# Attention's loads of q and keys issued by ScalarE, instead of SyncE, while q, k and v are made

## The chip, the core and the metric

The kernel runs on one core of one Trainium2 chip. A core has five engines with a program of their own each: TensorE (PE: matrix products into PSUM; its weight loads are the rows PEld), VectorE (DVE), ScalarE (ACT), GpSimd (POOL) and SyncE (SP), which only issues DMAs. An engine takes its instructions strictly in the order of its program. ACT and POOL issue some DMAs as well; such an issue stands in the engine's own program (ACTq, SPq in the profile), together with the waits that the issue needs. The metric is the time of one execution in microseconds, as the median of several runs.

## The reference

With x of 2048 positions by 640 features, float32 throughout:

```
xn  = layernorm(x)
qkv = xn @ wqkv                       # 640 x 1920; 32 heads of 20
logits[s, w] = q[s] . k[s - 2 w] / sqrt(20),  w = 0..7,  masked where s - 2 w < 0
o   = sum_w softmax_w(logits)[s, w] * v[s - 2 w]
s   = o @ wo                          # 640 x 640
g   = silu(((xn @ w_gate) * (xn @ w_up)) @ w_down)      # 640 -> 1536 -> 640
out = x + s * g
```

## The kernel before, in words

Products in float32 are made of three products of split values (a high part, rounded, and a low part), so that each tile of q, k, v takes 15 matmuls (three parts by five slices of 128 features). A split needs an instruction on ACT (line L114) and one on POOL (L115). PE does the products of all stages one behind the other; the other engines work beside it.

The 32 heads are cut into six groups of 6, 6, 4, 4, 6 and 6 heads, and the positions into two interleaved halves (`r` = 0, 1). A group of heads on one half of the positions is a *unit* of attention, `u = 2 * group + r`, twelve in all; they are worked off in the order 0, 1, 2, 3, 4, 6, 5, 7, 8, 11, 9, 10. Making q, k, v goes through five stages (`MADE`: the groups 0, 1, 2 with 3, 4, 5), eight tiles of 128 positions to a half. Function `qkv` makes one tile: 15 matmuls (L434) into a PSUM bank, then an *eviction* by ACT (L448) into a staging buffer (`s`, or `pk`); after every second tile, one DMA (L452) writes the buffer to a scratch tensor in HBM, `qkv_scr` of that unit, four such writes to a unit. From stage 1 on, ACT issues these writes. A matmul group may only begin in a bank when the last result in that bank has been evicted. While attention runs, the banks take turns: `q_one` (rows `q`), then one of two banks `g`, then one of two banks `u`. So `q_one` comes up again after three products, each `g` and `u` bank after six.

Attention is the generator `attention`, which DVE (products and sums: L542, L549, L508), POOL (sums of weighted values: L514) and ACT (the exponential L571, a copy of q L498) work off. A unit's data come from `qkv_scr` by DMAs: `load_kq(u)` loads q (L414) and the keys (L420, and two shifted parts, L422); `load_kv(u, 1)` loads the values in the same way. The keys are loaded one unit ahead: `ahead(n + 1, (0,))` asks for them as soon as the code that emits the program has emitted the last write of that unit. q has one buffer, `kv` two.

The order on every engine is that in which this code emits instructions; `advance` decides, by a budget of estimated times, how many steps of attention are emitted behind each product of another stage. Each DMA of SP and ACT takes one of eight completion semaphores in turn (`DMAHW0` to `DMAHW7` below) and waits first until the DMA before it on that semaphore has landed, whichever engine issued it.

Of the kernel before, what the change touches and what calls it, by code (L numbers as in the profile page):

```python
# [22 lines left out]
W, DIL = 8, 2  # L23
# [33 lines left out]
def kernel(  # L57
# [11 lines left out]
    nc = tc.nc  # L69
# [13 lines left out]
    def st(shape, tag, bufs, dt=F32):  # L83
        cnt[0] += 1
        pool = sb
        if tag == "gh":
            pool, bufs = gh_pool
        return pool.tile(shape, dt, tag=tag, bufs=bufs, name=f"{tag}_{cnt[0]}")
# [50 lines left out]
    def load_wq(g, parts, ahead={}):  # L139

        c3 = 3 * MC[g]
        wq_raw.setdefault(g, [])
        for p in parts:
            t = st([P, p[-1] - p[0], c3], "wraw", 2)
            for k0, k1 in zip(p, p[1:]):
                if k0 in ahead:
                    ahead[k0]()
                nc.sync.dma_start(t[:, k0 - p[0]:k1 - p[0]], wqkv[g][:, k0:k1, :])
                wq_raw[g].append((k0, k1, t[:, k0 - p[0]:k1 - p[0]]))
# [3 lines left out]
    def split_wq(g, eng, ks=(0, KD)):  # L153
        c3 = 3 * MC[g]
        if not fifth:
            fifth.append(slot([P, 4, 3 * 128]))
        if g not in wq and MC[g] > CMAX:
            y = [slot([P, 3, CH])[:, :, :c3] for _ in range(4)]
            wq[g] = [[y[n // 3][:, n % 3] for n in range(a * KD, a * KD + KD)] for a in range(2)]
            wq[g].append(None)  # L160
        elif g not in wq:
            cols = -(-c3 // 64) * 64
            hi, lo = (slot([P, KD - 1, cols])[:, :, :c3] for _ in range(2))
            wq[g] = [[y[:, k] for k in range(KD - 1)] + [fifth[0][:, g % 2 * 2 + a, :c3]] for a, y in enumerate((hi, lo))]
            wq[g].append((hi, lo))
        for k0, k1, t in wq_raw[g]:
            for a, b in ((k0, min(k1, KD - 1)), (max(k0, KD - 1), k1)):
                a, b = max(a, ks[0]), min(b, ks[1])
                if a < b:
                    if b - a > 1:  # L170
                        hi, lo = (y[:, a:b] for y in wq[g][2])
                    else:
                        hi, lo = (y[a].unsqueeze(1) for y in wq[g][:2])
                    split(eng, t[:, a - k0:b - k0], hi, lo)
# [3 lines left out]
    def load_wf(f):  # L178
        wf_raw[f] = slot([P, KD, 2, P], F32) if f == 0 else st([P, KD, 2, P], "wraw", 2)
        nc.sync.dma_start(wf_raw[f], wgu[f])  # L180
# [201 lines left out]
    q_t, kv_t, kv_buf, kv_zero, scr, staged, made = {}, {}, {}, {}, {}, [], set()  # L382

    def view_kv(u, b):

        c = GROUPS[UN[u][0]] * DH
        if b not in kv_buf:
            y = st([P, -(-2 * EXT * CMAX // 64) * 64], "kv", 2)
            kv_buf[b] = y[:, :2 * EXT * CMAX].rearrange("p (a x) -> p a x", a=2)
        kv_t[u] = kv_buf[b][:, :, :EXT * c].rearrange("p a (e c) -> p a e c", c=c)  # L390

    def zero_kv(u, b, a):

        if kv_zero.get((b, a)) != GROUPS[UN[u][0]]:
            nc.gpsimd.memset(kv_t[u][0:1, a, 0:W - 1, :], 0.0)
            kv_zero[b, a] = GROUPS[UN[u][0]]

    def begin_unit(m, r):
        for g in MADE[m]:
            u, c = 2 * g + r, GROUPS[g] * DH  # L400
            if u:
                scr[u] = dr.tile([P, 3, NE, c], F32, name=f"qkv_scr_{u}")
            else:
                q_t[u] = st([P, NE, c], "q", 1)
                view_kv(u, r)
                for a in range(2):
                    zero_kv(u, r, a)

    def load_kq(u):

        c, b = GROUPS[UN[u][0]] * DH, ORDER.index(u) % 2
        view_kv(u, b)
        q_t[u] = st([P, NE, c], "q", 1)
        nc.sync.dma_start(q_t[u], scr[u][:, 0])  # L414
        load_kv(u, 0)

    def load_kv(u, a):

        zero_kv(u, ORDER.index(u) % 2, a)
        nc.sync.dma_start(kv_t[u][:, a, W - 1:, :], scr[u][:, 1 + a])  # L420
        for p0, p1 in ((0, 112), (112, 127)):
            nc.sync.dma_start(kv_t[u][p0 + 1:p1 + 1, a, 0:W - 1, :], scr[u][p0:p1, 1 + a, 1:, :])  # L422

    ALL_RUNS = [(a, b, k) for a, b in ALL3 for k in range(KD)]

# [256 lines left out]
    def finish_piece():  # L682

        while unfinished:
            unfinished.pop(0)()
# [74 lines left out]
    def wd_sum(n):  # L760

        t = {name: w_scr[:, i] for i, name in enumerate(("T1", "T2", "T3", "T4"))}
        if n == 0:
            for name, b in (("T1", "B11"), ("T3", "B12"), ("T2", "B22"), ("T4", "B21")):
                nc.sync.dma_start(t[name], wd_block(b))
        else:
            out, y = ((t["T1"], wd_block("B12")), (t["T3"], wd_block("B22")), (t["T2"], t["T1"]), (t["T4"], t["T2"]))[n - 1]
            nc.gpsimd.dma_start(out, y, accum_op=ALU.add)
# [367 lines left out]
    def t_unit(j, a, k, c0=2):  # L1136

        if j == "T4":
            return xT[c0 + 1][a][:, k, :]
        n, i = T_UNIT[j, a, k] if c0 else divmod(T2_UNIT[j, a] + k, 3)  # L1140
        while len(tt[c0]) <= n:
            tt[c0].append(slot([P, 3, CH]))
        return tt[c0][n][:, i]

    def load_t(n):

        tt[0].append(slot([P, 3, CH]))
        nc.gpsimd.dma_start(tt[0][n], t_scr[:, 3 * n:3 * n + 3])
# [36 lines left out]
    def last_difference(k):  # L1185
        y = t4.pop(k)
        nc.scalar.activation(t_unit("T4", 0, k), y, AF.Copy)
        nc.gpsimd.tensor_sub(t_unit("T4", 1, k), y, t_unit("T4", 0, k).bitcast(F32))

    def step(n=1):  # L1190

        while n and steps:
            if next(steps[0], 0) == 0:
                steps.pop(0)
            else:
                n -= 1
# [18 lines left out]
    def w_split(f, *names):  # L1215

        for t in names:
            to, r = t, slice(0, W_ROWS[t])
            if t in "GU":
                y = wf_raw[f][:, :, "GU".index(t), :]  # L1220
                if t == "U" and two(f):
                    to, r, y = "R", slice(3, 6), y[:, 2:]
            else:
                y = w_sum[f][:, 6 * "SR".index(t):][:, :6 if t == "S" else 3]
                r = slice(0, 6 if t == "S" else 3)
            w_unit(f, {"G": "A11", "U": "A22", "S": "S1", "R": "S4"}[t])
            split(nc.gpsimd, y, tw[to][:, 0, r], tw[to][:, 1, r])
# [116 lines left out]
    def first_parts():  # L1344
        for name in ("S1", "S2", "S3", "d5", "S4"):
            w_add(2, name)
            yield
        w_split(2, "S")
        yield
# [6 lines left out]
    for m, t in ((m, t) for m in range(1, len(MADE)) for t in range(DIL)):  # L1356
        r = t if m < last else DIL - 1 - t
        begin_unit(m, r)
        heads, broad = MC[m] // DH, m < last and MC[m + 1] > CMAX
        for i in range(NE):  # L1360
            n = t * NE + i
            if m < last and n == 0:
                load_wq(m + 1, ((0, 2), (2, 4)) if broad else ((0, 3), (3, 5)))
            elif m < last and n in BLOCK:
                split_wq(m + 1, nc.gpsimd, (BLOCK.index(n), BLOCK.index(n) + 1))
            elif broad and n == BLOCK[1] + 1:
                load_wq(m + 1, ((4, 5),))
            if (m, r, i) == (last - 1, 1, 6):
                load_wf(2)
            if (m, n) in W_SUMS:  # L1370
                wd_sum(W_SUMS.index((m, n)))
            qkv(m, r, i)
            if m == last and n == NT - 7:
                staged[:] = [y for y in staged if y is not stage_pk[-1]]
            elif m == last and n == NT - 5:
                load_t(0)
            elif m == last and n == NT - 3:
                w_split(2, "G")
            if i == 1:
                finish_piece()  # L1380
            advance(PACE * heads * 0.38)
            paced += RATE[m - 1][t]
            while paced >= 1:
                paced -= 1
                step()
        if (m, r) == (last - 1, 1):
            steps.append(first_parts())
        elif (m, r) == (last, 1):
            for k in range(2):
                last_difference(k)  # L1390
    step(100)
    w_split(2, "R")
    w_sum.pop(2)
# [237 lines left out]
```

## Time and profile before

| | before |
|---|---|
| median of 3 runs (lowest to highest) | 736.02 us (735.68 to 736.02) |
| the profiled execution: its own time, its span from first to last instruction | 736.29 us, 734.4 us |
| PE busy, share of span | 728.2 us, 99% |
| DVE, POOL, ACT busy | 626.5, 450.5, 302.2 us |
| granted TensorE clock | 1.000 |
| DMA queue of SP (q1) / of ACT (q10) | 121.13 MB / 12.78 MB |

In a timeline row stand the start and the length in us, the engine, the source line, the operation, the tile written and those read, their sizes, and in brackets the idle time of the engine before it and what ended that. `SPq` and `ACTq` are DMA issues: their length is that of the issue, and the transfer follows. "To landing" is counted from the start of the issue to the completion.

### The profile page before, as it was taken

What the parts mean: (1) busy time and instruction counts of PE and PEld (TensorE: products, weight loads), DVE (VectorE), ACT (ScalarE), POOL (GpSimd) and SP (SyncE); (2) the same over time, 40 slices, a digit from 0 to 9 for tenths busy, and PEclk for the clock granted to TensorE, in tenths of its full rate; (3) what the DMA queues carried; (4) which work ended last, traced back from release to release, by engine and by line L of the source; (5) the groups of instructions that cost most, each with busy time, mean ns of one, the idle gap of its engine ahead of it and who ended that gap; (6) DMA issues with size and microseconds to landing.
All of it is one profiled execution on the core that took longest, in us unless ns stands there. A gap on an engine that the chain in (4) does not pass through costs nothing.

```text
span 734.4 us, 11062 instructions
## 1 busy us (share of the span) xinstructions
PE 728.2 (99%) x4030; PEld 666.0 (91%) x4030; DVE 626.5 (85%) x729; ACT 302.2 (41%) x561; POOL 450.5 (61%) x383
## 2 busy tenths in 40 slices
PE   8999999999999999999999999999999999999997
PEld 6989989988999998888888888888999999999997
DVE  7676998798796989899889999969899997777775
ACT  5668312323232333333233322334566664444442
POOL 6159919997779889797879969766644550000000
PEclk9999999999999999999999999999999999999999
DMA  8564588789767669462733542376768965555534
GB/s 325 170 204 158 208 303 300 239 256 257 190 193 164 220 204 323 141 180 87 221 88 105 177 141 68 80 218 183 208 211 241 315 236 194 194 194 194 194 108 143
DMA packets 106148, 143.78 MB, mean 196 GB/s; under 512 B 23048, under 2 KB 75524, under 8 KB 106094
## 3 DMA queue, kind: packets, MB, share of 16 engines
q1 hardware_dynamic: 88366, 121.13, 52.0%
q10 hardware_dynamic: 16000, 12.78, 5.4%
q0 software_dynamic: 1728, 9.18, 5.1%
q8 instruction: 31, 0.51, 0.3%
q14 instruction: 23, 0.19, 0.1%
HBM read 94.40 MB, written 55.67 MB: 204 GB/s over the span
## 4 chain that ended last, share of the span: by engine, by line
PE 98%; DMA 1%; DVE 0%; SPq 0%; ACT 0%; issue 0%
PE g L1292 16%; PE u L1292 11%; PE q L434 11%; PE q L866 9%; PE u L434 8%; PE g L434 8%; PE u L866 6%; PE q L1292 5%; PE u L124 5%; PE g L124 5%; PE q L996 3%; PE g L866 3%; PE e L866 3%; PE u L996 2%; PE e L996 2%; PE g L996 1%
## 5 line engine op out<-in xcount | busy, mean ns | idle before, releaser
L514 POOL TENSOR_TENSOR o<-o,t 128x960 f32<-128x960 f32 (+1 forms) x66 | 133.7, 2025 | 11.3 <-DVE t L508 10.1
L508 DVE TENSOR_TENSOR t<-e,kv 128x960 f32<-128x960 f32 (+1 forms) x96 | 99.6, 1038 | 21.1 <-POOL o L514 21.1
L542 DVE TENSOR_TENSOR t<-q,kv 128x1920 f32<-128x1920 f32 (+1 forms) x48 | 92.4, 1926 | 2.8 <-DMA kv<-qkv_scr 2.7
L549 DVE TENSOR_REDUCE lg<-t 128x96 f32<-128x1920 f32 (+1 forms) x48 | 92.3, 1923 | 0.2
L434 PE MATMUL q<-s,xc 128*128 128x360 f32 (+1 forms) x450 | 82.8, 334 | 0.5 <-DVE lg L272 0.5
L1261 ACT ACTIVATE gh<-g 128x512 f32<-128x512 f32 x57 | 34.2, 600 | 109.0 <-PE g L1292 108.1
L434 PEld LDWEIGHTS q<-s,xc 128*128 128x128 f32 x450 | 74.8, 188 | 4.6 <-DVE lg L272 0.7
L115 POOL TENSOR_TENSOR s<-wraw,s 128x384 fp32r<-128x384 f32 (+6 forms) x57 | 68.0, 1209 | 17.5 <-ACT s L114 17.5
L434 PE MATMUL u<-s,xc 128*128 128x360 f32 (+1 forms) x360 | 65.8, 334 | 0.0
L434 PEld LDWEIGHTS u<-s,xc 128*128 128x128 f32 x360 | 60.3, 188 | 2.3
L434 PE MATMUL g<-s,xc 128*128 128x360 f32 (+1 forms) x330 | 61.5, 337 | 0.0
L434 PEld LDWEIGHTS g<-s,xc 128*128 128x128 f32 x330 | 55.7, 188 | 2.6
L1292 PE MATMUL g<-s,s 128*128 128x512 f32 x228 | 57.9, 389 | 0.0
L1292 PE MATMUL u<-xc,s 128*128 128x512 f32 x228 | 57.9, 389 | 0.0
L866 PE MATMUL q<-xc,s 128*128 128x320 f32 x342 | 55.5, 309 | 0.0
L866 PEld LDWEIGHTS q<-xc,s 128*128 128x128 f32 x342 | 51.5, 188 | 0.0
L1292 PEld LDWEIGHTS g<-s,s 128*128 128x128 f32 x228 | 42.8, 188 | 8.9
L1292 PEld LDWEIGHTS u<-xc,s 128*128 128x128 f32 x228 | 42.8, 188 | 8.9
L114 ACT ACTIVATE s<-wraw 128x384 fp32r<-128x384 f32 (+6 forms) x58 | 32.6, 581 | 29.4 <-PE g L1292 10.2
L1292 PE MATMUL q<-xc,pk 128*128 128x512 f32 x171 | 41.9, 389 | 0.0
L1292 PE MATMUL g<-xc,s 128*128 128x512 f32 x171 | 41.9, 389 | 0.0
L514 POOL TENSOR_TENSOR o<-t 128x960 f32<-128x960 f32 (+1 forms) x11 | 22.1, 2011 | 27.4 <-DVE t L508 22.7
(328 smaller groups left out, 1559.7 us busy)
## 6 DMA issues: line engine op xcount, KB each, us to landing
h_scr<-gh SPq DMA_DIRECT2D x48, 256.0 KB, 2.8
wraw<-in_wgu SPq DMA_DIRECT2D x11, 640.0 KB, 4.8
kv<-qkv_scr SPq DMA_DIRECT2D x14, 480.0 KB, 6.1
t<-h_scr SPq DMA_DIRECT2D x8, 768.0 KB, 6.3
qkv_scr<-s ACTq DMA_DIRECT2D x17, 360.0 KB, 4.4
kv<-qkv_scr SPq DMA_DIRECT2D x14, 367.5 KB, 7.1
s_scr<-gh SPq DMA_DIRECT2D x16, 320.0 KB, 3.6
gh<-s_scr SPq DMA_DIRECT2D x16, 320.0 KB, 4.1
```

What stands on the lines that cost most here:

```text
L114: nc.scalar.activation(hi, raw, AF.Copy)
L115: eng.tensor_sub(lo, raw, hi.bitcast(F32))
L124: nc.tensor.matmul(acc, a, b, start=first and n == 0, stop=last and n == len(runs) - 1)
L434: nc.tensor.matmul(p, xT[(r * NE + i) // TPC][a][:, k, t0:t0 + P], wq[m][b][k], start=n == 0, stop=n == len(runs) - 1, skip_group_check=ac ...
L508: nc.vector.tensor_mul(t.rearrange("p (n d) -> p n d", d=DH), e[:, :, w].unsqueeze(2).to_broadcast([P, NE * nh, DH]), v)
L514: return NE * c * cost, lambda: eng.tensor_add(y, z, t)
L542: nc.vector.tensor_mul(t, q, k)
L549: nc.vector.tensor_reduce(out=lg[:, :, j:j + 2].rearrange("p n a -> p a n"), in_=t.rearrange("p a (n d) -> p a n d", d=DH), op=ALU.add, ax ...
L866: nc.tensor.matmul(p, y[:, i, k], wd_part(name, k, l), start=new and r == 0, stop=r == len(runs) - 1, skip_group_check=True)
L996: nc.tensor.matmul(b, y, w, start=new and r == 0, stop=r == len(runs) - 1, skip_group_check=True)
L1261: nc.scalar.activation(kept[j], b["ACACABA"[j]], AF.Copy)
L1292: nc.tensor.matmul(y, w, x, start=j in (0, 1, 5) and r == 0, stop=r == len(runs) - 1, skip_group_check=True)
```

## The change

Until q, k and v of all units are made, `load_kq` issues its four DMAs (q, and three for the keys) from ACT; after that from SP, as before. The loads of values stay on SP.

```diff
         q_t[u] = st([P, NE, c], "q", 1)
-        nc.sync.dma_start(q_t[u], scr[u][:, 0])
-        load_kv(u, 0)
+        by[0].dma_start(q_t[u], scr[u][:, 0])
+        load_kv(u, 0, by[0])
 
-    def load_kv(u, a):
+    by = [nc.scalar]
+
+    def load_kv(u, a, eng=nc.sync):
...
-        nc.sync.dma_start(kv_t[u][:, a, W - 1:, :], scr[u][:, 1 + a])
+        eng.dma_start(kv_t[u][:, a, W - 1:, :], scr[u][:, 1 + a])
         for p0, p1 in ((0, 112), (112, 127)):
-            nc.sync.dma_start(kv_t[u][p0 + 1:p1 + 1, a, 0:W - 1, :], scr[u][p0:p1, 1 + a, 1:, :])
+            eng.dma_start(kv_t[u][p0 + 1:p1 + 1, a, 0:W - 1, :], scr[u][p0:p1, 1 + a, 1:, :])
...
+    by[0] = nc.sync
     step(100)
```

It moves 28 DMA issues, four each for the units 1, 2, 3, 4, 6, 5 and 7, from SP's program to ACT's. The programs of PE, DVE and POOL are the same row for row. Lines of the kernel behind the diff stand two or three further down afterwards (L448 becomes L450, L452 becomes L454).

ACT's program where q, k, v of unit 2 are done: `qkv_scr_1147` is that unit's scratch, `g_1322`, `u_1350` and `q_1_68` are products in the banks g, u and `q_one`, `s_1319` is a split of another stage. Before:

```order
L1166 ACTIVATE s_1319<-gh_1175 128x512 [waits Pool_49]
L448 ACTIVATE s_798<-g_1322 128x3x120 [waits PE_49]
L452 DMA qkv_scr_1147<-s_798 384x1x240 [waits DMAHW0_49,Activation_49]
L114 ACTIVATE s_1226<-wraw_1150 128x480
L448 ACTIVATE s_798<-u_1350 128x3x120 [waits DMAHW3_49,PE_49]
L448 ACTIVATE s_798<-q_1_68 128x3x120 [waits PE_49]
```

And now, on the same engine at the same place:

```order
L1168 ACTIVATE s_1319<-gh_1175 128x512 [waits Pool_49]
L450 ACTIVATE s_798<-g_1322 128x3x120 [waits PE_49]
L454 DMA qkv_scr_1147<-s_798 384x1x240 [waits DMAHW0_49,Activation_49]
L414 DMA q_1340<-qkv_scr_1147 128x960 [waits DMAHW3_49,DMAHW5_49,DMAHW1_49,DMAHW0_49]
L422 DMA kv_128<-qkv_scr_1147 128x960 [waits DMAHW2_49]
L424 DMA kv_128<-qkv_scr_1147 112x840
L424 DMA kv_128<-qkv_scr_1147 15x840 [waits DMAHW4_49]
L114 ACTIVATE s_1226<-wraw_1150 128x480
L450 ACTIVATE s_798<-u_1350 128x3x120 [waits PE_49]
L450 ACTIVATE s_798<-q_1_68 128x3x120 [waits PE_49]
```

The four loads stand directly behind the unit's last write and ahead of a split and two evictions; the first of them waits for the four writes of the unit (DMAHW0 is that of the write just above it).

SP's program at unit 1, whose scratch is `qkv_scr_771`; `h_scr` takes results of the gate and up products, `wraw` weights. Before:

```order
L672 DMA h_scr<-gh_1030 128x4x128 [waits DMAHW3_49,DVE_49]
L414 DMA q_1034<-qkv_scr_771 128x960 [waits DMAHW4_49,DMAHW2_49,DMAHW1_49]
L420 DMA kv_1033<-qkv_scr_771 128x960 [waits DMAHW6_49,DMAHW5_49]
L422 DMA kv_1033<-qkv_scr_771 112x840
L422 DMA kv_1033<-qkv_scr_771 15x840 [waits DMAHW7_49]
L672 DMA h_scr<-gh_1077 128x4x128 [waits DMAHW0_49,DVE_49]
L672 DMA h_scr<-gh_1102 128x4x128 [waits DVE_49]
L148 DMA wraw_1148<-in_wqkv 128x960 [waits Pool_49]
```

And now:

```order
L674 DMA h_scr<-gh_1030 128x4x128 [waits DMAHW4_49,DVE_49]
L674 DMA h_scr<-gh_1077 128x4x128 [waits DMAHW0_49,DVE_49]
L674 DMA h_scr<-gh_1102 128x4x128 [waits DMAHW1_49,DVE_49]
L148 DMA wraw_1148<-in_wqkv 128x960 [waits DMAHW2_49,Pool_49]
L148 DMA wraw_1150<-in_wqkv 128x960 [waits DMAHW3_49,Pool_49]
```

The store of `gh_1077` no longer stands behind the four loads of unit 1; on ACT these stand between the evictions `gh_1028` and `gh_1075` of the gate products.

## The prediction

> **What bounds the kernel now.** I read the page first, then the waits of PE.
>
> ```profile
> PE 728.2 (99%) x4030; PEld 666.0 (91%) x4030; DVE 626.5 (85%) x729; ACT 302.2 (41%) x561; POOL 450.5 (61%) x383
> PEclk9999999999999999999999999999999999999999
> PE 98%; DMA 1%; DVE 0%; SPq 0%; ACT 0%; issue 0%
> PE q L229 <- POOL lg masks.py:199: 1.4, 1, 1.4
> PE q L434 <- DVE lg L272: 0.5, 1, 0.5
> ```
>
> The first row is busy time by engine, the second the granted clock by slice, the third the shares of the chain that ended last, and the last two are all the waits of PE in the execution. PE is the chain, at full clock, and it waits for nobody but in its first microseconds. So a change on ACT and SP has nothing to shorten: SP's waits and ACT's idle time lie beside PE. What it can do is make PE wait where it did not, and as PE is dense to the end, such a wait is kept in full. The question is whether ACT, which now waits for loads' conditions in its own program, evicts a bank too late. The tightest bank is `q_one`, which comes up every third product.
>
> **Unit 2, the place that decides.** ACT's timeline, then SP's, then PE's:
>
> ```profile
> 122.40 0.47 ACT L448 ACTIVATE s<-q 128x360 f32<-128x360 f32 x1 [0.72 <-PE q L434]
> 129.19 0.63 ACT L1166 ACTIVATE s<-gh 128x512 fp32r<-128x512 f32 x1 [6.32 <-POOL gh L1162]
> 129.73 0.45 ACT L448 ACTIVATE s<-g 128x360 f32<-128x360 f32 x1
> 130.21 0.52 ACTq L452 DMA_DIRECT2D qkv_scr<-s  x1
> 130.78 0.60 ACT L114 ACTIVATE s<-wraw 128x480 fp32r<-128x480 f32 x1 [0.60 <-ACT s L448]
> 131.29 0.46 ACT L448 ACTIVATE s<-u 128x360 f32<-128x360 f32 x1
> 131.64 0.46 ACT L448 ACTIVATE s<-q 128x360 f32<-128x360 f32 x1
> ...
> 133.24 0.33 SPq L414 DMA_DIRECT2D q<-qkv_scr  x1
> 133.62 0.69 SPq L420 DMA_DIRECT2D kv<-qkv_scr  x1
> 134.36 0.92 SPq L422 DMA_DIRECT2D kv<-qkv_scr  x2
> ...
> 127.00 2.56 PE L434 MATMUL q<-s,xc 128*128 128x360 f32 x15
> 129.40 2.56 PE L434 MATMUL g<-s,xc 128*128 128x360 f32 x15
> 131.80 2.56 PE L434 MATMUL u<-s,xc 128*128 128x360 f32 x15
> 134.20 2.56 PE L434 MATMUL q<-s,xc 128*128 128x360 f32 x15
> ...
> DMA to landing us min/median/max: 3.0/3.0/3.0
> ```
>
> The last row is that of the write at 130.21: it lands at 133.2, and there SP issues the load of q, at 133.24. ACT is already late here: it stood 6.32 us for a sum of POOL, and catches up with three evictions in a row. The eviction of `q_one` ends at 131.64 + 0.46 = 132.10, and PE begins the next product in that bank at 134.20, so the slack is 2.10 us.
>
> Now the four loads stand behind the write at 130.21. ACT waits for the same landing, 133.24, and issues: on SP the four took from 133.24 to 134.36 + 0.92 = 135.28, 2.04 us. What began at 130.78 begins at about 135.33, 4.55 us later; the `q_one` eviction ends at 136.65 and PE starts at 136.65 rather than 134.20: **2.45 us of PE time lost**, 4.55 - 2.10. The bank `g` and `u` products in between have slack of six products and stay. The price of an issue on ACT is bounded by rows of its own: ACT's write above took 0.52, so four are 2.1; at SP's least, 0.33 each, 1.3. I take SP's 2.04 and keep -0.7 to +0.6 for the range.
>
> Behind the eviction, the exponential of attention comes some 2.8 us later too; DVE waited there anyway for keys, and PE has moved by about as much, so I cost it at nothing. If that cover goes, attention runs late; PE has no wait for it anywhere in the rows above.
>
> **Unit 1 sets when ACT gets there.** SP, ACT, DVE and POOL around it:
>
> ```profile
> 96.41 0.33 SPq L414 DMA_DIRECT2D q<-qkv_scr  x1
> 98.27 2.43 SPq L672 DMA_DIRECT2D h_scr<-gh  x2
> ...
> 95.40 0.60 ACT L657 ACTIVATE gh<-g 128x512 f32<-128x512 f32 x1 [6.20 <-PE g L124]
> 99.78 0.50 ACT L571 ACTIVATE e<-lg 128x384 f32<-128x384 f32 x1 [3.78 <-DVE lg L569]
> ...
> 95.19 0.68 DVE L668 TENSOR_TENSOR gh<-u,gh 128x512 f32<-128x512 f32 x1
> 103.08 2.16 DVE L542 TENSOR_TENSOR t<-q,kv 128x1920 f32<-128x1920 f32 x1 [1.12 <-DMA kv<-qkv_scr]
> 109.50 2.27 POOL L514 TENSOR_TENSOR o<-t 128x960 f32<-128x960 f32 x1 [14.80 <-DVE t L508]
> ...
> h_scr<-gh SPq DMA_DIRECT2D x48, 256.0 KB, 2.8
> kv<-qkv_scr SPq DMA_DIRECT2D x14, 480.0 KB, 6.1
> kv<-qkv_scr SPq DMA_DIRECT2D x14, 367.5 KB, 7.1
> q<-qkv_scr SPq DMA_DIRECT2D x7, 480.0 KB, 5.5
> ```
>
> ACT now stands until 96.4, when the last write of unit 1 has landed, issues until about 98.4, and evicts at 98.4 what it evicted at 95.40. That gate result lies in one of two `g` banks, and ACT is free at 99.0, before the exponential's 99.78: no cost. But SP no longer stands behind the loads: its store of the product that DVE ended at 95.87 goes out at 95.9, not at 98.27, beside the loads. DVE began unit 1 when these had landed, at 103.08, after 1.12 us of waiting, and POOL's chain up to the sum that ACT waits for at 129.19 starts from there. The loads are 1,328 KB in these rows, and took from 96.41 to 103, some 200 KB/us; 256 KB ahead of them cost up to 1.2 us, if all of it shares their time. At the other end, in a queue of their own, they could land sooner, of which DVE can use 1.12 us. I take +0.5, nearer to the first since the bytes are certain, and each microsecond counts in full at 134.20. That makes 2.45 + 0.5 = 2.95.
>
> **Unit 3, the other wait.**
>
> ```profile
> 145.17 0.52 ACTq L452 DMA_DIRECT2D qkv_scr<-s  x1
> 151.10 4.39 ACTq L452 DMA_DIRECT2D qkv_scr<-pk  x2
> 160.05 3.42 PE L434 MATMUL q<-s,xc 128*128 128x480 f32 x15
> DMA to landing us min/median/max: 11.6/11.6/11.6
> ```
>
> The last write of unit 3, at 145.17, landed after 11.6 us. The loads stand behind the two writes at 151.10, which go out about as before. With PE 2.95 later, the write is issued at about 147.6 and lands by 159.2; ACT is through with the issues at 161.3, has evicted `q_one` (0.57) by 161.9, and PE asks for the bank at 163.0. Slack 1.1 us: no cost, but near.
>
> **Units 4, 6, 5 and 7** are asked for in ACT's program behind the last write of their half, later than SP had issued the loads; the first and the last of the four, and DVE's first use of the last:
>
> ```profile
> 178.40 0.34 SPq L414 DMA_DIRECT2D q<-qkv_scr  x1
> 183.60 1.20 ACTq L452 DMA_DIRECT2D qkv_scr<-s  x2
> ...
> 255.18 0.34 SPq L414 DMA_DIRECT2D q<-qkv_scr  x1
> 263.70 0.52 ACTq L452 DMA_DIRECT2D qkv_scr<-s  x1
> 276.79 1.48 DVE L542 TENSOR_TENSOR t<-q,kv 128x1280 f32<-128x1280 f32 x1
> ```
>
> SP's conditions were met before ACT arrives, so these groups wait for nothing. Unit 7's loads slip by 12 us, to some 267 with PE 2.95 later, and need 5 to 7 us to land; DVE asks at 276.8. Four issues hold ACT for 2.04 us, while a `q_one` eviction has two products, 4.8 us. No cost. What SP gains, some 14 us of issuing and shorter queues for its stores, value loads and weights, has no waiter on PE: no gain. POOL's DMAs stay where they are.
>
> **Sum.** 2.45 + 0.5 = 2.95 us. The profiled execution took 736.29 (span 734.4), 0.27 above the median 736.02; on the median it gives **739.0 us**.
>
> **Rivals.**
> - *The stall is covered (not slower).* ACT is idle 59% of the time, and if it gets to unit 2's write earlier, the issues fit. Place: the 6.32 us wait for POOL ahead of 129.19. Price: loads of unit 1 in their own queue land 1.12 us sooner, and issues at SP's least take another 0.7 off: 2.45 - 1.8 = 0.6, 736.6. It decides where ACT's delay at the `q_one` eviction is under 2.1 + 1.5 us. Against it: SP's store now goes beside these loads.
> - *Only the issuer differs (not slower).* PE would show no wait and the time 736.0, if ACT held nothing back behind a waiting DMA. Against it: the row at 151.10, where two issues of ACT take 4.39 us. The Trainium skill has this as a rule, in "DMA: Bandwidth & Descriptors", section "Issuing engines are not separate DMA queues": DMAs of all engines run interleaved on the same 16 DMA engines, and the choice of issuer only saves its issue time, usually small. By that rule alone the change is worth nothing.
> - *Two stalls.* The write of unit 3 lands 2.6 us later than I have it (it then shares q10 with more loads): PE waits another 1.5 us, 740.5; with the upper ends at unit 2 (1.2 - 0.5 and 0.6) 741.8. The clock could add to it: "TensorE: Matmul & The Clock Gate", Part 1, in the Trainium skill, has the clock halved after an idle window of about 3.4 us; no run here shows it, and a gap of 2.95 is under it.
> - *Faster.* SP's earlier stores would have to end a wait of PE, and it has none after the start: 735 at best.
>
> **How the numbers follow.** One stall: 0.60, from 2.45 - 0.7 - 1.1 = 0.6 to 2.45 + 0.6 + 1.2 = 4.2 us, mostly within 737.5 to 740.2. The two covered rivals 0.09 each, two stalls 0.18, faster 0.04. A measurement can tell about 0.2%, 1.5 us. Slower by more: 0.56 of the first and the 0.18, 0.74; within: 0.04 and 0.18, 0.22; faster: 0.04. The range leaves out the lower covered cases and the upper part of two stalls: 736.5 to 741.5.
>
> **What would show it.** PE with one wait of 2 to 4 us for ACT's L450 at a product into `q_one` near 134; ACT with four issues behind the write near 130; PE's later rows shifted by the same amount; no waits at units 4 to 7. Wrong would be: PE without a wait, a second one near 163, or the wait of DVE at 103 gone.

## The result, and the profile after

| | before | after |
|---|---|---|
| median (lowest to highest) | 736.02 us (735.68 to 736.11, 4 runs) | 743.38 us (741.67 to 744.72, 4 runs) |
| the profiled execution: time, span | 736.29, 734.4 us | 744.14, 742.4 us |
| DMA queue of SP / of ACT | 121.13 / 12.78 MB | 113.14 / 20.77 MB |

The changed kernel is slower: ratio 1.010, 95% interval 1.0076 to 1.0123. The forecast of 739.0 us had the direction and the place, but 743.4 lies above its range (736.5 to 741.5).

The page of the kernel after (busy time), and all the waits of PE:

```profile
PE 732.5 (99%) x4030; PEld 669.8 (90%) x4030; DVE 628.1 (85%) x729; ACT 301.7 (41%) x561; POOL 451.5 (61%) x383
...
PE q L436 <- ACT s L450: 3.9, 1, 3.9
PE q L229 <- POOL lg masks.py:199: 1.4, 1, 1.4
PE q L436 <- DVE lg L272: 0.2, 1, 0.2
```

One wait of PE is new, 3.9 us for the eviction L450. But the span is 8.0 us longer, and PE's busy time grew by 4.3: about half of the loss isn't idle time, so a list of waits shows only the other half. PE's timeline at that wait, and seventy us later:

```profile
131.60 2.56 PE L436 MATMUL u<-s,xc 128*128 128x360 f32 x15
138.02 4.26 PE L436 MATMUL q<-s,xc 128*128 128x360 f32 x15 [3.86 <-ACT s L450]
142.07 2.69 PE L436 MATMUL g<-s,xc 128*128 128x360 f32 x15
...
204.02 2.63 PE L436 MATMUL q<-s,xc 128*128 128x360 f32 x15
206.49 2.63 PE L436 MATMUL g<-s,xc 128*128 128x360 f32 x15
```

From start to start, a product of 360 columns took 2.40 us in the kernel before (127.00, 129.40, 131.80). Here the one behind the gap begins 6.42 us after its predecessor, 4.02 too late; it takes 4.05 us (138.02 to 142.07), 1.65 too long; and all later ones take 2.47 (204.02 to 206.49), to the last of them. That is 164.4 ns for each matmul, not 160.0; with 35 products of 15 it makes 35 x 15 x 4.4 ns = 2.3 us. The sum is 4.0 + 1.65 + 2.3 = 8.0 us. The granted clock explains most of the second term (window in us, its length, then busy time of PE, PEld, DVE, ACT and POOL, PEclk, DMA share, GB/s):

```profile
136.00:138.00 2.00, 0.00 (x0) 0.00 (x0) 0.35 (x1) 1.32 (x3) 0.68 (x1) 1.00 0.85 292
138.00:139.00 1.00, 0.98 (x5) 0.99 (x6) 0.00 (x0) 0.44 (x1) 1.00 (x2) 0.89 1.02 417
139.00:140.00 1.00, 1.00 (x5) 1.00 (x5) 0.06 (x1) 1.00 (x4) 1.00 (x1) 0.50 1.07 330
140.00:142.07 2.07, 2.07 (x8) 2.07 (x8) 2.00 (x4) 0.82 (x2) 1.99 (x2) 0.50 0.67 203
142.07:144.60 2.53, 2.53 (x16) 2.53 (x16) 2.50 (x2) 0.47 (x1) 2.53 (x3) 0.98 0.64 209
```

The clock falls to half about 0.8 us after PE has started again, stays there for some 3.4 us, and is full afterwards: the slower 2.47 us are not the clock. The 40-slice row of the page still shows 9 everywhere; the dip is too short for it.

ACT's timeline at the place, to be held against the one of before:

```profile
130.17 0.63 ACT L1168 ACTIVATE s<-gh 128x512 fp32r<-128x512 f32 x1 [7.15 <-POOL gh L1164]
130.71 0.45 ACT L450 ACTIVATE s<-g 128x360 f32<-128x360 f32 x1
131.19 0.52 ACTq L454 DMA_DIRECT2D qkv_scr<-s  x1
134.80 0.35 ACTq L414 DMA_DIRECT2D q<-qkv_scr  x1
135.19 0.44 ACTq L422 DMA_DIRECT2D kv<-qkv_scr  x1
135.65 0.94 ACTq L424 DMA_DIRECT2D kv<-qkv_scr  x2
136.64 0.60 ACT L114 ACTIVATE s<-wraw 128x480 fp32r<-128x480 f32 x1 [5.48 <-issue]
137.15 0.45 ACT L450 ACTIVATE s<-u 128x360 f32<-128x360 f32 x1
137.50 0.46 ACT L450 ACTIVATE s<-q 128x360 f32<-128x360 f32 x1
```

It is the forecast stall: behind the write ACT waits 3.6 us for the landing, issues for 1.84 us, and evicts `q_one` by 137.96, while PE had been ready for that bank since 134.0.

### The profile page after: what moved, and what is told of

The parts are those of the page before. It is cut to its first block, busy times and chain, and to the rows that moved or that the text cites. A ratio compares the mean times of both kernels' runs of the same rounds, so it can differ in the third digit from the quotient of the medians.

```text
span 742.4 us, 11051 instructions
## 1 busy us (share of the span) xinstructions
PE 732.5 (99%) x4030; PEld 669.8 (90%) x4030; DVE 628.1 (85%) x729; ACT 301.7 (41%) x561; POOL 451.5 (61%) x383
## 3 DMA queue, kind: packets, MB, share of 16 engines
q1 hardware_dynamic: 85244, 113.14, 48.0%
q10 hardware_dynamic: 19122, 20.77, 8.6%
## 4 chain that ended last, share of the span: by engine, by line
PE 90%; DVE 3%; POOL 2%; DMA 2%; issue 1%; ACT 0%; SPq 0%; ACTq 0%; POOLq 0%; DVEq 0%
PE g L1294 16%; PE u L1294 10%; PE q L436 9%; PE q L868 9%; PE u L436 7%; PE g L436 6%; PE u L868 6%; PE q L1294 5%; PE u L124 3%; PE g L124 3%; PE q L998 3%; PE g L868 3%; PE e L868 3%; PE u L998 2%; PE e L998 2%; DVE lg L551 1%
## 5 line engine op out<-in xcount | busy, mean ns | idle before, releaser
L436 PE MATMUL q<-s,xc 128*128 128x360 f32 (+1 forms) x450 | 85.6, 341 | 4.1 <-ACT s L450 3.9
L436 PEld LDWEIGHTS q<-s,xc 128*128 128x128 f32 x450 | 77.0, 191 | 8.7 <-ACT s L450 4.1
L115 POOL TENSOR_TENSOR s<-wraw,s 128x384 fp32r<-128x384 f32 (+6 forms) x57 | 68.5, 1220 | 23.1 <-ACT s L114 23.1
L114 ACT ACTIVATE s<-wraw 128x384 fp32r<-128x384 f32 (+6 forms) x58 | 32.6, 581 | 35.0 <-issue 10.9
```

Source lines behind the costliest of these rows:

```text
L114: nc.scalar.activation(hi, raw, AF.Copy)
L115: eng.tensor_sub(lo, raw, hi.bitcast(F32))
L436: nc.tensor.matmul(p, xT[(r * NE + i) // TPC][a][:, k, t0:t0 + P], wq[m][b][k], start=n == 0, stop=n == len(runs) - 1, skip_group_check=ac ...
```

## The experiments

The eviction is line L448 of the kernel before, L450 of the changed one, and L451 or L459 in variants of it. The runs of before beside these had medians of 735.98 to 736.25 us.

**The change again, and its parts.** The changed kernel once more:

> The changed kernel as it is, for a second profile. Theory (one stall, then a halved clock for one window, then a slower pace of 360-column products): a PE wait near 4 us at the same product, 741 to 745; whether clock and pace come every time is open, and the runs' scatter of 3 us, where before scatters 0.4, suggests that one of them does not. If neither came, 740; rival (a fixed cost of the second queue): each run the same within 0.5.

Measured: 744.52 us (744.09 to 745.55), ratio 1.0116 (1.0101 to 1.0131). Its profiled execution had a gap of 4.2 us and two clock windows rather than one (half from 136.9 to 143.8). Only unit 2's loads on ACT:

```diff
-        by[0].dma_start(q_t[u], scr[u][:, 0])
-        load_kv(u, 0, by[0])
+        eng = nc.scalar if u == 2 else nc.sync
+        eng.dma_start(q_t[u], scr[u][:, 0])
+        load_kv(u, 0, eng)
```

> Only unit 2's four loads are issued by ScalarE; those of the other six units are back on SyncE. Theory (one stall): the whole loss hangs on this one place. ScalarE reaches the write at about 130.2 as before, waits 3.0 to 3.6 us for it to land, issues for 1.8 us, so PE stands 2.2 to 2.8 us for the q_one eviction; that alone gives 738.2 to 738.8, and if such a gap also halves the clock (1.6 us) and leaves the 360-column products at the slower pace (2.3 us), up to 742.7. Rival (all seven groups, or the second queue, cost a little each): a seventh of the loss, about 737. Second rival (unit 1's part is the larger): no PE wait over 1 us, 736 to 737.

Measured: 742.70 us (741.35 to 746.52), ratio 1.0098 (1.007 to 1.0126). Four of the 28 issues make a loss as large as that of all. The converse, all groups but unit 2's (`by[0] if u != 2 else nc.sync`):

> ScalarE issues the loads of units 1, 3, 4, 6, 5 and 7; unit 2's four are back on SyncE. Theory (one stall): no PE wait after the start, clock 1.0 throughout, 360-column products 160 ns apart, 736.0 within 0.5. Rival (all seven groups, or the second queue, cost a little each): six sevenths of the loss, 741 to 743, with a slower pace of PE while ScalarE's loads run.

Measured: 738.68 us, ratio 1.0034 (1.0024 to 1.0044), in two groups: 736.05 and 736.28, and eight runs from 738.3 to 739.84. The profile is of one of the former, without any wait of PE, but ACT at unit 3 in it is close (PE asks for the bank at 160.09):

```profile
158.89 0.57 ACT L451 ACTIVATE s<-q 128x480 f32<-128x480 f32 x1 [7.78 <-DMA qkv_scr<-pk]
...
160.09 3.42 PE L437 MATMUL q<-s,xc 128*128 128x480 f32 x15
```

Only q's load of unit 2 on ACT, its keys on SP (`load_kv(u, 0)` without the engine):

> Of the 28 loads only unit 2's q is issued by ScalarE; its keys and all other loads are on SyncE. Theory (one stall, made of a wait and four issues): ScalarE waits for the write to land, 3.0 to 3.6 us, and issues once for 0.35, so it is 2.8 to 3.4 us late; less the slack of 2.1 us PE stands 0.7 to 1.3 us: 736.7 to 737.3, without a drop of the clock. If any restart of PE can leave the 360-column products at the slower pace, 2.3 us more: up to 739.6. Rival (the issues themselves are the cost): no PE wait, 736.0.

Measured: 739.39 us (736.48 to 742.59), ratio 1.0044 (1.0027 to 1.0061). PE's timeline of its profiled run (739.46):

```profile
131.77 2.56 PE L437 MATMUL u<-s,xc 128*128 128x360 f32 x15
134.85 2.74 PE L437 MATMUL q<-s,xc 128*128 128x360 f32 x15 [0.52 <-ACT s L451]
137.43 2.63 PE L437 MATMUL g<-s,xc 128*128 128x360 f32 x15
```

A gap of 0.5 us with the clock full all the time (1.00 in each window), and yet 3.2 us lost: the products run 2.47 us apart from there on. So the slower pace needs no clock drop, and a gap of half a microsecond was enough to set it here.

**A gap with no DMA moved.** In the kernel before, copies that nobody reads stand on ACT behind unit 2's last write. 14, 22 and 30 of them:

```diff
                 if i == NE - 1:
                     made.add(2 * g + r)
+                if (m, r, i) == (1, 0, NE - 1):
+                    for _ in range(14):
+                        nc.scalar.activation(st([P, 1], "exp", 1), eps_t, AF.Copy)
```

> As the long one with 14 such copies: ScalarE is held 2.83 us, so PE should wait 0.7 us. Theory A: too short for the clock, so 736.0 + 0.7 + 2.3 = 739.0, products of 360 columns 164.4 ns apart behind the gap, as when q's load alone was moved. Theory B: 736.7, products 160.0 ns apart throughout.

> All loads on SyncE; 22 copies that nobody reads behind unit 2's last write, between the 14 and the 30 of the earlier kernels, whose gaps were 1.05 and 4.69 us: 0.2275 us for each copy, so a gap of 2.9 us, the size that the prediction had for the change. If the clock is halved only by a gap of 3.4 us, as the prediction took it: 736.1 + 2.9 + 2.2 (slower products) = 741.2 in every run. If a shorter gap can do it, by how its windows fall: some or all runs 1.5 to 1.7 us above that, 742.7 to 743, with a product of some 4.1 us behind the gap.

> All loads on SyncE, as in the kernel before; behind the last write of unit 2 stand 30 copies of one column on ScalarE (0.20 us each in the trace of before, 6.06 us) that nobody reads. They hold ScalarE as long as the four loads did, with no DMA moved. With 2.10 us of slack PE should wait 4.0 us at the product of 134.2. Theory A (a gap of PE brings the clock's halving and the slower 360-column products by itself, whatever makes it): 736.0 + 4.0 + 1.7 to 3.4 (clock) + 2.3 (products 164.4 ns apart instead of 160.0) = 742.5 to 746. Theory B (the slow products come from loads in ScalarE's queue, beside its writes): 740.0 with products 160.0 ns apart and at most the clock's share on top, 740 to 743.4.

| copies | gap of PE | median (lowest to highest) | ratio, interval | product behind the gap |
|---|---|---|---|---|
| 14 | 1.05 us | 739.82 us (737.47 to 740.0) | 1.0044 (1.0029 to 1.0059) | 2.58 us |
| 22 | 2.91 us | 743.51 us (741.86 to 744.08) | 1.0096 (1.0079 to 1.0112) | 3.98 us |
| 30 | 4.69 us | 745.46 us (743.04 to 746.54) | 1.0120 (1.0098 to 1.0142) | 4.52 us |

The rows of PE behind the gap, of 14, of 22 and of 30 copies:

```profile
135.38 2.74 PE L434 MATMUL q<-s,xc 128*128 128x360 f32 x15 [1.05 <-ACT s L448]
137.96 2.63 PE L434 MATMUL g<-s,xc 128*128 128x360 f32 x15
140.43 2.63 PE L434 MATMUL u<-s,xc 128*128 128x360 f32 x15
```

```profile
136.92 4.18 PE L434 MATMUL q<-s,xc 128*128 128x360 f32 x15 [2.91 <-ACT s L448]
140.90 2.77 PE L434 MATMUL g<-s,xc 128*128 128x360 f32 x15
```

```profile
139.16 4.68 PE L434 MATMUL q<-s,xc 128*128 128x360 f32 x15 [4.69 <-ACT s L448]
143.68 2.63 PE L434 MATMUL g<-s,xc 128*128 128x360 f32 x15
```

With every load on SP, a gap of PE gives the same three terms: itself, the slower products, and in the two longer ones the clock. The loads in ACT's queue are not needed for any of them. The lowest run with 14 copies, 737.47, has no profile; it may be one without the slower products. A gap of 2.91 us, the forecast one, halves the clock:

```profile
134.20:137.00 2.80, 0.08 (x1) 0.08 (x1) 0.88 (x2) 2.48 (x10) 1.33 (x2) 1.00 0.94 317
137.00:139.00 2.00, 2.00 (x9) 2.00 (x10) 0.15 (x1) 1.53 (x4) 2.00 (x2) 0.70 1.04 330
139.00:141.00 2.00, 2.00 (x9) 2.00 (x8) 1.93 (x4) 0.72 (x2) 1.92 (x2) 0.50 0.31 106
```

**Which other units cost.** Unit 3 alone (`u == 3`), the four units 4 to 7 (`u in (4, 5, 6, 7)`), and all but 2 and 3 (`by[0] if u not in (2, 3) else nc.sync`; unit 8's loads, which that expectation names, were on SP in every kernel):

> Only unit 3's four loads are issued by ScalarE. In the kernel with all groups but unit 2's moved, ScalarE had evicted q_one at 159.46 and PE asked at 160.09: 0.63 us to spare. Theory A: that slack is near zero from run to run, as the write of unit 3 lands after 11.6 us, now earlier, now later; times fall in two groups, 736.0 to 736.3 without a wait and 738 to 740 with a small one and slower products behind it (32 of them, 2.1 us), mean ratio 1.002 to 1.004. The rival (unit 1's or units 4 to 7's loads cost those 2.6 us): 736.0 in all runs.

> Only the loads of units 4, 6, 5 and 7 are issued by ScalarE, 16 of the 28. Theory A (all of the loss starts at units 2 and 3): 736.0, no wait of PE, products 160.0 ns apart, same as before within 0.1%. The rival (each group costs a little on ScalarE): 737 to 739.

> The loads of units 1, 4, 6, 5, 7 and 8 stay on ScalarE, those of units 2 and 3 go back to SyncE. Theory (what costs is the eviction of q_one held up at units 2 and 3): no wait of PE, products 160.0 ns apart, 736.0 to 736.3 in every run, though unit 1's loads still land beside SyncE's store and ScalarE comes later at 129. The rival (unit 1's move costs by itself, the +0.5 of the prediction and more; or loads in ScalarE's queue do): 736.5 to 738.

Units 4 to 7: 736.08 us (735.81 to 736.72), ratio 1.000 (0.9991 to 1.001). All but 2 and 3: 735.93 us (735.76 to 736.38), ratio 1.000 (0.9991 to 1.0009). Both run at 160.0 ns to the end. Twenty of the 28 issues cost nothing. Unit 3 alone: 738.59 us, ratio 1.0029 (1.0016 to 1.0041), in two groups, 736.46 and 736.54, and five runs from 738.53 to 739.77. This time the profile (738.97) is of a slower run; ACT's and PE's rows:

```profile
156.61 0.36 ACTq L415 DMA_DIRECT2D q<-qkv_scr  x1
157.00 1.62 ACTq L423 DMA_DIRECT2D kv<-qkv_scr  x1
158.66 1.17 ACTq L425 DMA_DIRECT2D kv<-qkv_scr  x2
159.87 0.57 ACT L451 ACTIVATE s<-q 128x480 f32<-128x480 f32 x1 [8.78 <-DMA q<-qkv_scr]
...
160.49 3.53 PE L437 MATMUL q<-s,xc 128*128 128x480 f32 x15 [0.27 <-ACT s L451]
...
198.83 2.63 PE L437 MATMUL q<-s,xc 128*128 128x360 f32 x15
201.30 2.63 PE L437 MATMUL g<-s,xc 128*128 128x360 f32 x15
```

The four issues took 3.22 us here (156.61 to 159.83), not 1.83 as in the all-but-unit-2 run above (157.01 to 158.84): ACT is late by a quarter of a microsecond. The products of 480 columns keep their pace but for the first, and when those of 360 columns come again, 36 us after the gap, they are 2.47 us apart. A wait of 0.3 us cost 2.7 (738.97 against 736.3).

**A gap at the end of the products.** 26 copies ahead of the last eviction of `q_one` but one among the 360-column products (`if (m, r, i) == (4, 0, 4)`, ahead of the activation), so that one such product is left behind the gap:

> All loads on SyncE; 26 copies of one column that nobody reads (0.234 us each in the trace with 30 of them, 6.1 us) stand in ScalarE's program ahead of the last but one eviction of q_one among the 360-column products, so that PE waits about 1.2 us with one such product left. Theory (a gap slows the 360-column products behind it, and nothing else): 736.1 + 1.2 + 0.07 = 737.4. The rival (a gap of this size costs some 2.5 us more wherever it lies, as the short copies at unit 2 did: 3.7 in all for a wait of 1.05): 739.8.

Measured: 738.89 us (738.4 to 739.13), ratio 1.0034 (1.0021 to 1.0048), so neither number. PE's rows:

```profile
270.33 2.67 PE L434 MATMUL q<-s,xc 128*128 128x360 f32 x15 [0.40 <-ACT s L451]
272.84 1.55 PE L1295 MATMUL g<-xc,pk 128*128 128x512 f32 x6
...
280.45 0.50 PE L1295 MATMUL u<-xc,s 128*128 128x512 f32 x1 [0.82 <-POOL s L115]
```

The gap was 0.4 us only. The product behind it took 2.51, but not at the slower pace: in the trace its second matmul starts 269 ns after the first, and all the others 160 ns apart. In the run with q's load alone the matmuls behind the gap of 0.5 start 270 ns apart, then 163 to 170. So a gap doesn't always set the slower pace. What made up the rest were two more waits: a split of weights, which ACT (L114) does behind the held-up evictions and POOL (L115) finishes, was late by 0.8, and at 290.72 PE waited 0.4 for a DMA. The test is weak on size, since the delay went another way than planned. That the slower pace isn't carried over to the stage of 512 columns is seen elsewhere: in the changed kernel that stage ran at 227 ns per matmul, as before, behind products of 164.4.

**The loads on ACT, but behind the eviction.** If only the eviction held up counts, ACT can keep all 28 issues where each group is written behind the next eviction of `q_one`:

```diff
-        by[0].dma_start(q_t[u], scr[u][:, 0])
-        load_kv(u, 0, by[0])
+        zero_kv(u, b, 0)
+        pend.append(u)
+        if by[0] is nc.sync:
+            flush()
...
+            if bank[0] == "q" and ring[turns[0] % len(ring)] is q_one:
+                flush()
```

Here `flush` issues what is pending; it also runs ahead of `copy_q`.

> All 28 loads stay in ScalarE's program, but each group is written behind the next eviction of q_one rather than ahead of it. At unit 2 ScalarE evicts q_one at about 132.1 as before, then waits for the write's landing (133.2) and issues until 135.3; the next bank it owes PE is wanted some 4 us later. Theory (only the eviction held up counts, not the queue, not the issuing): no wait of PE, products 160.0 ns apart, 736.0 to 736.3 in all runs, same as before. The rival (loads in ScalarE's queue cost something by themselves): 737 or more.

Measured: 743.63 us (743.53 to 745.09), ratio 1.0100 (1.0083 to 1.0117): a miss. Unit 1 has no such eviction near, so its loads went out 3.3 us later, at 99.67. DVE, ACT and PE then:

```profile
109.88 2.16 DVE L556 TENSOR_TENSOR t<-q,kv 128x1920 f32<-128x1920 f32 x1 [8.22 <-DMA kv<-qkv_scr]
...
125.43 0.63 ACT L1180 ACTIVATE s<-gh 128x512 fp32r<-128x512 f32 x1 [10.06 <-POOL gh L1176]
...
128.88 2.74 PE L445 MATMUL q<-s,xc 128*128 128x360 f32 x15 [2.02 <-ACT s L459]
...
138.91 4.28 PE L445 MATMUL q<-s,xc 128*128 128x360 f32 x15 [2.35 <-ACT s L459]
```

DVE's late start makes POOL's sums late, ACT stands for them, and PE waits twice ahead of any load of unit 2. The second variant issues unit 1's loads at once (`if u == 1 or by[0] is nc.sync`):

> As the kernel before this one (all 28 loads in ScalarE's program, each group behind the next eviction of q_one), but unit 1's four, which have no such eviction near and were issued at 99.67 rather than 96.33 there, go out at once, as in the changed kernel. DVE should then not wait 8.22 us for unit 1's keys, nor ScalarE for POOL's sums behind them. Theory (only the eviction held up counts): no wait of PE behind 120 us, products 160.0 ns apart, 736.0 to 736.5. The rival (loads in ScalarE's queue cost something by themselves): 738 or more again.

Measured: 747.97 us (745.93 to 749.23), ratio 1.0156 (1.0142 to 1.017), the slowest of all. ACT's rows, SP's and PE's:

```profile
147.74 0.52 ACTq L465 DMA_DIRECT2D qkv_scr<-pk  x1
148.31 0.47 ACT L459 ACTIVATE s<-q 128x360 f32<-128x360 f32 x1 [8.70 <-DMA kv<-qkv_scr]
...
142.07 0.44 SPq L431 DMA_DIRECT2D kv<-qkv_scr  x1
...
148.83 4.87 PE L445 MATMUL q<-s,xc 128*128 128x360 f32 x15 [7.38 <-ACT s L459]
```

At unit 2 itself all went as planned: no wait of PE at 134.09, `q_one` evicted ahead of the loads. But the moved issues renumber the completion semaphores that the DMAs take in turn, and a write of unit 3 on ACT now shares one (DMAHW4) with SP's load of unit 2's values. That load is issued at 142.07; the write, wanted from about 139.6, waits until it has landed, to 147.74, and the next eviction of `q_one` stands behind it. So this version was not shown to be free; that loads on ACT cost nothing by themselves is shown by the twenty of units 1 and 4 to 7.

## Why the prediction was wrong

The sum had one term, a wait of PE of 2.95 us. The profiled run lost 8.0 us: a wait of 4.0, 1.65 more in the product behind it, most of it by the clock, and 2.3 in the slower products after that. So place and mechanism of the wait were right, its size was not, and what follows a wait was priced at nothing.

- **PE is the chain, only a wait of PE counts: right, but not the whole.** No other engine's delay counts, as the two kernels without a wait of PE show (736.08, 735.93). Missing was that PE itself can get slower behind a wait.
- **Unit 2 decides, `q_one`, near 134, ACT behind the landing: right** in place, bank and mechanism, and the four issues (1.84 us against 2.04 taken).
- **The size of the stall, 2.95 us: mis-sized, 4.0 measured.** ACT came to the write 1.2 us later relative to PE, not 0.5, and the write landed after 3.6 us, not 3.03; less 0.2 for the issues that is the whole 1.05. In the profiles ACT's arrival there varied from -0.2 to +1.2 us: +0.8 with unit 1's loads on SP (unit 2 alone), +0.2 with them on ACT (all but 2 and 3). So the +0.5 can't be put down to unit 1's loads, as the prediction did; the landing varied from 3.1 to 4.5 us. Both were taken from one execution as if they were fixed. The +0.6 that the range keeps for the issues has no row behind it: four at 0.52 us are 2.1, which is 0.06 over the 2.04.
- **The clock dismissed, since "a gap of 2.95 is under it": the step that failed in principle.** 2.91 us halved the clock, and so did 2.35 (product 4.11 us, behind a first gap of 2.02 that didn't). The Trainium skill, "TensorE: Matmul & The Clock Gate", Part 1, also says that the window is free-running; I had used the 3.4 us and not this. The traces agree: in the changed kernel the clock changed at 138.78 and 142.20 us, 3.41 apart, and the stretches at full clock before and after lasted 133.12 and 600.75, 39 and 176 times that, from a start that differed from execution to execution. Halved stretches are one or two such windows long (3.4 us, or 6.8 in the repeat). From full clock, every window of this grid in which PE had stood 2.19 us or more was followed by a halved one (2.19 with 30 copies, 133.25 to 136.66), and none with 1.91 or less (1.91 in the last variant, 139.95 to 143.37). So a gap of 2.95 us can halve the clock or not, as the windows cut it. The product behind the gap took 1.65 us too long in the profiled run; with 14 copies, where the clock stayed full, it was 0.18, so the clock's part is some 1.5 us.
- **"Such a wait is kept in full": too little.** The slower products behind the wait, 2.3 us here, were in none of the terms. They are the largest part of what the prediction left out altogether, and they alone account for most of the loss of the runs with short gaps.
- **Unit 3 "no cost, but near": half right.** In the changed kernel PE had no wait there, since PE itself came 5.7 us later; with unit 2 on SP it was decided from run to run, within the slack of 0.6 us.
- **Units 4, 6, 5, 7 and SP's relief, nothing: right** (ratio 1.000 in both kernels).
- **The rivals.** "Only the issuer differs" holds where PE needs nothing soon of what stands behind the loads: at unit 1 ACT stood 7.0 us for the landing in its own program (all but 2 and 3), and it cost nothing. So the Trainium skill's rule in "DMA: Bandwidth & Descriptors" agrees with the twenty issues of units 1 and 4 to 7, and not with the four of unit 2 or those of unit 3. "Two stalls" came nearest (740.5 to 741.8), still below the 743.4 and for the wrong reason: PE had one stall. "Faster" and "covered" did not occur.

## What to carry to other kernels

A DMA issued by a compute engine puts its wait for data into that engine's program: ask what the engine owes to PE behind it, and whether the slack there exceeds landing plus issues, with the spread of both. Where PE is dense, price a gap of PE as more than itself, by the products that follow it: gaps of 0.3 and 0.5 us cost 2.7 and 3.2 here. And look up the completion semaphores after each move of a DMA, as two DMAs that have nothing to do with each other can come to share one.

## What the runs showed that was not expected

- Behind a gap of as little as 0.3 us, 15 matmuls of 128x360 took 2.47 us, not 2.40 (164.4 against 160.0 ns each), to the last of the 360-column products, at full clock, in every profile with such a gap at unit 2 or 3 (ten of ten), but not behind the gap of 0.4 us at 270. Products of 480 columns in between kept their 3.25 us, and matmuls of 320 and 512 columns 147 and 227 ns.
- The same two paces stand in the first microseconds, where the program of PE is the same in all kernels. In 14 of the 15 profiles, not in that of the kernel before, the two 360-column products at 19 to 24 us took 2.47 us, and in all 15 those from 35 us on took 2.40. Between them lie products of 256 and 512 columns. So the slower pace can also end; what sets or restores it isn't shown. In the changed kernel:

```profile
21.50 2.63 PE L436 MATMUL e<-s,xc 128*128 128x360 f32 x15
23.97 1.95 PE L124 MATMUL g<-xc,s 128*128 128x256 f32 x15
...
34.66 2.56 PE L436 MATMUL q<-s,xc 128*128 128x360 f32 x15
37.06 2.56 PE L436 MATMUL e<-s,xc 128*128 128x360 f32 x15
```

- The granted clock fell to 0.50 behind or during gaps of 2.35, 2.91, 3.86, 4.2, 4.6, 4.7 and 7.4 us, and not behind 0.3, 0.4, 0.5, 1.05 and 2.02.
- Two kernels (all but unit 2, unit 3 alone) fell into two groups of times 2 us apart (736.0 to 736.5, and 738.3 to 739.8) with nothing between. The one profile of the lower group has no wait of PE behind the first microseconds, the one of the upper a wait of 0.3 us and the slower pace behind it: a few tenths of a microsecond at one bank decided over the pace of the whole stage.
